# Hashed attention with two MLP layers: weight blocks converted and split in pairs of 1024 columns

## Chip, cores and metric

The kernel runs on one core of a Trainium2 chip. The metric is the device time of one launch in microseconds (us), the median of several runs. Engines are called TensorE (PE in the rows), VectorE (DVE), ScalarE (ACT), GpSimd (POOL) and SyncE (SP, whose queue issues all large DMAs here).

## What is computed

Attention in which a query sees only the keys of its hash bucket, then two MLP layers on the result. B, H, S, D are 2, 8, 768, 64; there are 6 hash bits, 1536 tokens, a model width of 512 and a hidden width of 2048.

```
q_bits = (q @ proj) > 0;  k_bits = (k @ proj) > 0
mask   = bucket(q_bits) == bucket(k_bits)
p      = softmax(where(mask, q @ k.T / sqrt(64), -1e9))
x      = heads_side_by_side(p @ v)                         # 1536 x 512
x      = relu(x @ w_in)**2 @ w_out                         # layer 0
h      = x @ w_in2
out    = (max(h, 0) + alpha * min(h, 0)) @ w_out2          # layer 1
```

The four weight matrices are float64 on the host and reach the kernel as their 64 bits.

## The kernel before

**Tiling.** Tokens are handled in NCH = 4 chunks of 384, and the hidden width in KFF = 16 steps of 128. A work item is a layer, a chunk and a step, 128 in all; `feed_forward` runs the 16 steps of a layer and chunk. A step needs two weight blocks of 128x512: block 0, from `w_in`, for the hidden product (`hidden`: 12 matmuls of 384 columns), and block 1, from `w_out`, for the projection (`project`: 9 matmuls of 512 columns). The projection of step f-1 is written behind the hidden product of step f. [...]

**The way of a weight block.** `load_bits` loads the raw 64-bit words as a tile `wbits` (two 32-bit words per value). `to_f32` makes float32 of it: ScalarE scales the high words into a tile `we` (L502), VectorE masks the sign into `wsg` (L504), adds bits of the low word (L505) and puts exponent and mantissa in place (L507). The result goes to a float32 tile `wf` (`fetch`, for layer 0 in its first chunk) or stays in `we` (`ahead`, for layer 1), and is stored to a scratch tensor in DRAM, from where later chunks load it again (L554). `split_w` then copies the high part on ScalarE (L528) and subtracts it on VectorE or GpSimd (L529). In layer 1 `keep` brings the blocks back into SBUF for good.

**Overlap.** Attention of the first chunk is computed first. Attention of chunk c+1 runs as background steps between the matmuls of layer 0 on chunk c, and the conversion of the layer 1 weights runs beside chunks 1 and 2 of layer 0. From about 480 us on there is no attention any more, only layer 0 on the last chunk and layer 1 (the late stage). In the attention each tile of scores is two pairs of matmuls into PSUM (L350, L351); VectorE takes its row maximum (L354), ScalarE the exponential (L357) that frees the PSUM tile. `recip` and `finish` scale the result by the row sums: `rrow` goes through DRAM and comes back as `rb`, and VectorE multiplies (`x`, L414), ScalarE makes `xh` (L415).

**What sets the order.** A list scheduler fixes, when the kernel is built, the order of instructions on each engine from the order of the code and its own estimates. At run time each engine and the SyncE queue work strictly in that order and wait on semaphores. A tile is taken from a pool with a fixed number of buffers; a new tile waits until the last reader of the buffer's earlier one is done. Pools that matter here: `whole` 4 (`wf`), `conv` 1 (`we` and `wsg`), `parts0` 2 and 3 in the late stage, `parts1` 2 (`wh`, `wl` of each block), `wide` 3 and 8 in the late stage (`wbits`, late `wf`).

**A step in the code.** `feed_forward` splits block 0 of the next item and block 1 of this one, computes the hidden product, fetches float32 weights two items ahead, loads raw bits three items ahead, and projects. GpSimd makes `wl` for each block 1 and, in the second chunk of layer 0, for block 0 too (`o or i // KFF == 1`); VectorE makes the rest.

Of the kernel before, what the change touches and what calls it, by code (L numbers as in the profile page):

```python
# [29 lines left out]
def kernel(  # L30
# [20 lines left out]
    nc = tc.nc  # L51
    B, H, D, S = qT.shape
    NB = N_BITS
    NT, DM = out.shape
    P = 128
    T = S // 2
# [20 lines left out]
    m2 = pool("m2", 2)  # L77
    state_whole = pool("whole", 4)
    weights = ctx.enter_context(ExitStack())
# [37 lines left out]
    def f32(ap):  # L117
        return ap.bitcast(F32)


    GR = 32
# [8 lines left out]
    def constants():  # L130
# [4 lines left out]
        with tc.tile_pool(name="once", bufs=1) as once:  # L135
            first = tc.keep_in_program_order
            cols = once.tile([P, D], i32, name="cols")
            row = once.tile([P, 1], i32, name="row")
            bit = once.tile([P, 1], i32, name="bit")
# [3 lines left out]
            sign = once.tile([P, D], F32, name="sign")  # L143
            nc.gpsimd.iota(row, [[0, 1]], base=0, channel_multiplier=1)
# [9 lines left out]
            first(nc.vector.tensor_tensor(of, of, above, ALU.mult))  # L154
            first(nc.vector.tensor_scalar(bit, row, GR // 2 - 1, None, ALU.bitwise_and))
            first(nc.vector.tensor_scalar(cols, cols, bit, 1, ALU.logical_shift_right, ALU.bitwise_and))
            first(nc.vector.tensor_scalar(sign, cols, 2.0, -1.0, ALU.mult, ALU.add))
# [6 lines left out]
            first(nc.vector.tensor_scalar(nb[:, 0, :], nb[:, 0, :], 1, None, ALU.bitwise_and))  # L164
            ones = once.tile([P, NB], F32, name="ones")
            first(nc.vector.tensor_copy(ones, nb[:, 0, :]))
# [38 lines left out]
    class Pair:  # L205
# [100 lines left out]
        def q_ids(self):  # L306
# [178 lines left out]
    w_d = {}  # L485
    kept = {}
    y_d = {}

    def load_bits(u):
        l, f, o = u  # L490
        t = state["wide"].tile([P, DM, 2], U32, tag="wide", name="wbits")
        nc.sync.dma_start(out=t.rearrange("p n b -> p (n b)"), in_=(WO if o else WI)[l][f].bitcast(U32))
        w_bits[u] = t

    def to_f32(u, w=None):


        if u not in w_bits:
            load_bits(u)
        t = w_bits.pop(u)  # L500
        e = state["conv"].tile([P, DM], F32, tag="we", name="we")
        nc.scalar.activation(e, t[:, :, 1].bitcast(F32), AF.Copy, scale=2.0 ** -112)  # L502
        s = state["conv"].tile([P, DM], U32, tag="wsg", name="wsg")
        nc.vector.tensor_scalar(s, t[:, :, 1], 0x80000000, None, ALU.bitwise_and)  # L504
        nc.vector.scalar_tensor_tensor(s, t[:, :, 0], 29, s, ALU.logical_shift_right, ALU.bitwise_or)  # L505
        w = e if w is None else w
        nc.vector.scalar_tensor_tensor(  # L507
            w.bitcast(U32), e.bitcast(U32), 3, s, ALU.logical_shift_left, ALU.bitwise_or
        )
        return w  # L510

    def ahead(u):

        w = to_f32(u)
        w_d[u] = dram.tile([P, DM], F32, tag="w%d_%d_%d" % u, name="w%d_%d_%d" % u)
        nc.sync.dma_start(out=w_d[u], in_=w)

    def keep(u):

        kept[u] = state["res"].tile([P, DM], F32, name="w%d_%d_%d" % u)  # L520
        nc.sync.dma_start(out=kept[u], in_=w_d[u])

    def split_w(u, engine):
        w = w_f.pop(u)
        o = u[2]
        hi = state["parts%d" % o].tile([P, DM], F32R, tag=f"wh{o}", name=f"wh{o}")
        lo = state["parts%d" % o].tile([P, DM], F32R, tag=f"wl{o}", name=f"wl{o}")
        nc.scalar.activation(hi, w, AF.Copy)  # L528
        engine.tensor_tensor(lo, w, f32(hi), ALU.subtract)  # L529
        w_split[u] = (hi, lo)  # L530
# [4 lines left out]
    def units(i):  # L535

        if i >= len(work):
            return []
        l, c, f = work[i]
        return [(l, f, o) for o in range(2)]  # L540

    def fetch(i):

        for u in units(i):
            if u in kept:
                w_f[u] = kept[u]
            elif u in w_d:
                if state["attention"]:
                    w = state["whole"].tile([P, DM], F32, tag="wf", name="wf")
                else:  # L550

                    w = state["wide"].tile([P, DM, 2], U32, tag="wide", name="wf")
                    w = w.rearrange("p n b -> p (n b)")[:, 0:DM].bitcast(F32)
                nc.sync.dma_start(out=w, in_=w_d[u])  # L554
                w_f[u] = w
            else:
                w_f[u] = state["whole"].tile([P, DM], F32, tag="wf", name="wf")
                to_f32(u, w_f[u])
                w_d[u] = dram.tile([P, DM], F32, tag="w%d_%d_%d" % u, name="w%d_%d_%d" % u)
                nc.sync.dma_start(out=w_d[u], in_=w_f[u])  # L560

    def split(i, o):
        for u in units(i)[o:o + 1]:
            split_w(u, nc.gpsimd if o or i // KFF == 1 else nc.vector)

# [58 lines left out]
    def feed_forward(l, c, background):  # L624
# [11 lines left out]
        for f in range(KFF):  # L636
            i = index[l, c, f]
            split(i + 1, 0)
            split(i, 1)
            g = hidden(l, c, f, x, step)  # L640
            fetch(i + 2)
            for u in units(i + 3):
                if u not in w_d and u[0] == 0:
                    load_bits(u)
# [60 lines left out]
    for f in range(KFF):  # L705
        for o in range(2):
            steps += [lambda u=(1, f, o): load_bits(u), lambda u=(1, f, o): ahead(u)]

# [97 lines left out]
```

## Time and profile before

| | us |
|---|---|
| median of 3 runs (lowest to highest) | 852.25 (851.3 to 853.84) |
| the profiled execution | 850.58 |
| its span in the trace | 848.8 |
| TensorE busy in the span | 798.8 (94%) |
| VectorE busy | 504.0 (59%) |
| ScalarE busy | 470.5 (55%) |
| GpSimd busy | 359.6 (42%) |

The profile is one execution, 1.67 us below the median of the runs; 1.8 us of it lie around the span. A row of the profile names a line of the kernel, the engine, the operation, the output and inputs with shapes, and a count. "Idle before" is the time for which the engine did nothing directly before an instruction, and the arrow names what ended it. The granted clock is the share of its full speed at which TensorE ran.

### The profile page before, as it was taken

The numbers are of one execution on the slowest core, as the hardware profiler recorded it, in microseconds if no ns is written. First come the engines' busy times: TensorE is split into PE (matmuls) and PEld (weight loads), VectorE is DVE, ScalarE is ACT, GpSimd is POOL, SyncE is SP. The second block draws the span as 40 slices with busy tenths as digits, with TensorE's granted clock in tenths as the row PEclk, the third lists the DMA queues.
The fourth block names the chain that finished last, engine by engine and source line by source line (L and its number), as shares of the span: only waits on it lengthen the run. The fifth ranks groups of instructions, "written<-read, shape, count | busy, mean of one in ns | idle before, by whom it ended". The sixth has DMA issues, their size and how long they took to land.

```text
span 848.8 us, 12785 instructions
## 1 busy us (share of the span) xinstructions
PE 798.8 (94%) x4384; PEld 648.0 (76%) x4384; DVE 504.0 (59%) x819; ACT 470.5 (55%) x919; POOL 359.6 (42%) x315
## 2 busy tenths in 40 slices
PE   3988799999999989999989999999999999999997
PEld 1656486767787666677677789989989998998996
DVE  6576789998567567788888431224435445444442
ACT  3566587777575655565565556654434443444332
POOL 1000232323555565533333355545555555555553
PEclk9999799999999999999999999999999999999999
DMA  7567767777867767778775489600101011000001
GB/s 206 153 174 214 226 229 249 239 252 249 228 215 215 236 192 240 234 245 257 241 219 170 120 310 314 233 29 10 38 1 37 1 38 38 1 1 37 1 1 38
DMA packets 62096, 130.09 MB, mean 153 GB/s; under 512 B 8816, under 2 KB 21072, under 8 KB 62032
## 3 DMA queue, kind: packets, MB, share of 16 engines
q1 hardware_dynamic: 62032, 129.28, 48.6%
q8 instruction: 35, 0.57, 0.3%
q14 instruction: 29, 0.24, 0.1%
HBM read 83.32 MB, written 23.12 MB: 125 GB/s over the span
## 4 chain that ended last, share of the span: by engine, by line
PE 48%; DVE 7%; DMA 3%; issue 2%; ACT 2%; POOL 1%; SPq 0%; POOLq 0%; DVEq 0%; ACTq 0%
PE acc L608 7%; PE acc L604 7%; PE acc L605 7%; PE m L578 4%; PE m L576 4%; PE m L577 4%; PE h L576 3%; PE h L577 3%; PE h L578 3%; PE m L387 3%; DMA w<-we 2%; DVE low L354 1%; DVE wsg L504 1%; DVE we L507 1%; DVE pt L377 1%
## 5 line engine op out<-in xcount | busy, mean ns | idle before, releaser
L594 POOL TENSOR_TENSOR gl<-g,gh 128x384 fp32r<-128x384 f32 x128 | 136.1, 1063 | 246.0 <-ACT gh L593 123.2
L604 PE MATMUL acc<-wh,gh 128*128 128x512 f32 x384 | 158.2, 412 | 0.0
L529 POOL TENSOR_TENSOR wl<-wf,wh 128x512 fp32r<-128x512 f32 x80 | 108.4, 1356 | 112.8 <-ACT wh L528 102.5
L605 PE MATMUL acc<-wl,gh 128*128 128x512 f32 x384 | 152.1, 396 | 0.0
L528 ACT ACTIVATE wh<-w 128x512 fp32r<-128x512 f32 x128 | 80.5, 629 | 80.8 <-PE m L577 45.6
L608 PE MATMUL acc<-wh,gl 128*128 128x512 f32 x384 | 115.8, 398 | 2.1 <-POOL gl L594 2.1
L528 ACT ACTIVATE wh<-wf 128x512 fp32r<-128x512 f32 x128 | 80.5, 630 | 64.8 <-PE h L577 24.2
L576 PE MATMUL h<-xh,wh 128*128 128x384 f32 x296 | 106.7, 360 | 4.6 <-ACT xh L415 3.2
L354 DVE TENSOR_REDUCE low<-s 128x1 f32<-128x768 f32 x84 | 80.1, 953 | 38.0 <-PE s L351 37.8
L577 PE MATMUL h<-xl,wh 128*128 128x384 f32 x296 | 101.6, 343 | 0.4 <-POOL xl L416 0.4
L578 PE MATMUL h<-xh,wl 128*128 128x384 f32 x296 | 101.5, 343 | 0.0
L357 ACT ACTIVATE sm<-s,low 128x768 f32<-128x768 f32 x84 | 75.6, 900 | 37.5 <-DVE low L354 37.1
L608 PEld LDWEIGHTS acc<-wh,gl 128*128 128x128 f32 x384 | 71.5, 188 | 21.3 <-POOL gl L594 5.0
L371 PE MATMUL m<-ident,sm 128*128 128x128 f32 x525 | 82.9, 276 | 4.0 <-ACT sm L357 1.8
L529 POOL TENSOR_TENSOR wl<-w,wh 128x512 fp32r<-128x512 f32 x64 | 82.7, 1291 | 6.0 <-ACT wh L528 6.0
L604 PEld LDWEIGHTS acc<-wh,gh 128*128 128x128 f32 x384 | 72.4, 189 | 15.9 <-issue 5.7
L605 PEld LDWEIGHTS acc<-wl,gh 128*128 128x128 f32 x384 | 72.5, 189 | 9.2 <-issue 0.6
L593 ACT ACTIVATE gh<-g 128x384 fp32r<-128x384 f32 x64 | 33.5, 524 | 81.7 <-DVE g L592 81.7
L591 DVE TENSOR_SCALAR r<-m,alpha_sb 128x384 f32<-128x384 f32 x43 | 26.6, 618 | 87.0 <-PE m L578 86.7
L371 PEld LDWEIGHTS m<-ident,sm 128*128 128x128 f32 x525 | 64.1, 141 | 18.5 <-ACT sm L357 3.0
L350 PE MATMUL s<-k,q 128*128 128x384 f32 x168 | 63.9, 380 | 12.6 <-ACT sm L357 10.6
L578 PE MATMUL m<-xh,wl 128*128 128x384 f32 x216 | 73.0, 338 | 0.5 <-DVE wl L529 0.5
(112 smaller groups left out, 1475.2 us busy)
## 6 DMA issues: line engine op xcount, KB each, us to landing
wf<-w SPq DMA_DIRECT2D x96, 256.0 KB
wbits<-in_w_in_dram SPq DMA_DIRECT2D x32, 512.0 KB
wbits<-in_w_out_dram SPq DMA_DIRECT2D x32, 512.0 KB
w<-wf SPq DMA_DIRECT2D x32, 256.0 KB
w<-we SPq DMA_DIRECT2D x32, 256.0 KB
w<-w SPq DMA_DIRECT2D x32, 256.0 KB
q<-qh SPq DMA_DIRECT2D x60, 96.0 KB
k<-kh SPq DMA_DIRECT2D x28, 192.0 KB
```

What stands on the lines that cost most here:

```text
L354: nc.vector.tensor_reduce(low, ps[:, 0:2, 0:HALF], AX.XY, ALU.max, negate=True)
L357: nc.scalar.activation(sm.rearrange("p (a n) -> p a n", a=2), ps[:, 0:2, 0:HALF], AF.Exp, bias=low, accum_out=self.sums[:, i:i + 1],)
L371: nc.tensor.transpose(ps[:, i * P:(i + 1) * P], pp[:, b * P:(b + 1) * P], ident)
L528: nc.scalar.activation(hi, w, AF.Copy)
L529: engine.tensor_tensor(lo, w, f32(hi), ALU.subtract)
L576: nc.tensor.matmul(hp, wih[:, ks], xh[:, kk, :], start=first, stop=False)
L577: nc.tensor.matmul(hp, wih[:, ks], xl[:, kk, :], start=False, stop=False)
L578: nc.tensor.matmul(hp, wil[:, ks], xh[:, kk, :], start=False, stop=last)
L594: nc.gpsimd.tensor_tensor(gl, g, f32(gh), ALU.subtract)
L604: nc.tensor.matmul(acc[:, t, :], gh[:, blocks[t]], woh, start=first, stop=False)
L605: nc.tensor.matmul(acc[:, t, :], gh[:, blocks[t]], wol, start=False, stop=False)
L608: nc.tensor.matmul(acc[:, t, :], gl[:, blocks[t]], woh, start=False, stop=last)
```

## The change

Block 1 of item i and block 0 of item i+1 become one pair, held in one tile of 128x2x512.

- `to_f32` and `wh` work on 1024 columns in one operation: 31 conversions of pairs and two of single blocks, 126 `wh` copies of pairs and four of single blocks. The subtractions for `wl` stay 512 columns wide, the second half of the tile (block 0 of i+1) first.
- There is no tile `we`. ScalarE scales the high words in place in `wbits`, and VectorE's first operation reads them after that. A result of `ahead` stays in `wsg` and is stored from there.
- Fetching is one item ahead and not two, raw bits two and not three. Loads and stores are as many and as large as before.
- Pools hold pairs: `whole` 2, `parts` 2 (early and late), `wide` 2 and 8 late, `conv` one `wsg`.
- `ql` is written over `qn`, and three tiles of `constants` over others.

Lines of the changed kernel: L505 scaling, L507, L508 and L510 the three VectorE operations, L578 `wh`, L585 `wl`, L352 the row maximum, L412 `x`, L401 `rrow`, L615 `gh`.

```diff
-    state_whole = pool("whole", 4)
+    state_whole = pool("whole", 2)
...
-        state["parts0"] = pool(f"parts0{late}", 2 + late, stack)
-        state["parts1"] = pool(f"parts1{late}", 2, stack)
-        state["wide"] = pool(f"wide{late}", 8 if late else 3, stack)
+        state["parts"] = pool(f"parts{late}", 2, stack)
+        state["wide"] = pool(f"wide{late}", 8 if late else 2, stack)
...
-            ql = p1.tile([P, T], F32R, tag="ql", name="ql")
+            ql = self.qn.bitcast(F32R)
...
+    def load_bits(us):
+        t = state["wide"].tile([P, 2, DM, 2], U32, tag="wide", name="wbits")
+        for k, (l, f, o) in enumerate(us):
+            nc.sync.dma_start(
+                out=t[:, k].rearrange("p n b -> p (n b)"), in_=(WO if o else WI)[l][f].bitcast(U32)
+            )
+        w_bits[us] = t
+
+    def to_f32(us, w=None):
...
+        e = t[:, 0:n, :, 1]
+        nc.scalar.activation(e.bitcast(F32), e.bitcast(F32), AF.Copy, scale=2.0 ** -112)
+        s = state["conv"].tile([P, 2, DM], U32, tag="wsg", name="wsg")[:, 0:n]
+        nc.vector.tensor_scalar(s, e, 0x80000000, None, ALU.bitwise_and)
+        nc.vector.scalar_tensor_tensor(s, t[:, 0:n, :, 0], 29, s, ALU.logical_shift_right, ALU.bitwise_or)
+        w = s if w is None else w.bitcast(U32)
+        nc.vector.scalar_tensor_tensor(w, e, 3, s, ALU.logical_shift_left, ALU.bitwise_or)
+        return w.bitcast(F32)
+
+    def store(us, w):
+        for k, u in enumerate(us):
+            w_d[u] = dram.tile([P, DM], F32, tag="w%d_%d_%d" % u, name="w%d_%d_%d" % u)
+            nc.sync.dma_start(out=w_d[u], in_=w[:, k])
+
+    def ahead(us):
+        store(us, to_f32(us))
...
+    def fetch(i):
+        us = blocks_of(i)
...
+        ring = "whole" if state["attention"] else "wide"
+        w = state[ring].tile([P, 2, DM], F32, tag=ring, name="wf")
+        new = bits_of(i)
+        if len(new) == 2:
+            to_f32(us, w)
+            store(us, w)
...
+    def split(i):
+        us = blocks_of(i)
+        w, parts = w_f.pop(i)
+        hi = state["parts"].tile([P, 2, DM], F32R, tag="wh", name="wh")
+        lo = state["parts"].tile([P, 2, DM], F32R, tag="wl", name="wl")
+        if parts is None:
+            nc.scalar.activation(hi, w, AF.Copy)
...
+        for k, u in reversed(list(enumerate(us))):
+            engine = nc.gpsimd if u[2] or i // KFF == 1 else nc.vector
+            engine.tensor_tensor(lo[:, k], parts[k], f32(hi[:, k]), ALU.subtract)
...
-            split(i + 1, 0)
-            split(i, 1)
+            split(i)
             g = hidden(l, c, f, x, step)
-            fetch(i + 2)
-            for u in units(i + 3):
-                if u not in w_d and u[0] == 0:
-                    load_bits(u)
+            if i + 1 < len(work):
+                fetch(i + 1)
+            if i + 2 < len(work) and bits_of(i + 2) and state["attention"]:
+                load_bits(bits_of(i + 2))
...
+    fetch(-1)
     fetch(0)
-    fetch(1)
-    split(0, 0)
+    split(-1)
```

The change moves instructions in three places. First, VectorE ahead of the first `x` of the MLP (behind the last `rrow` of the first chunk); before:

```order
L529 TENSOR_TENSOR wl_1028<-wf,wh_1027 128x512
L504 TENSOR_SCALAR wsg<-wbits 128x512
L505 SCALAR_TENSOR_TENSOR wsg<-wbits,wsg 128x512
L507 SCALAR_TENSOR_TENSOR wf<-we,wsg 128x512
L504 TENSOR_SCALAR wsg<-wbits 128x512
L235 TENSOR_SCALAR bits<-m 128x96
L505 SCALAR_TENSOR_TENSOR wsg<-wbits,wsg 128x512
L235 TENSOR_SCALAR bits<-m 128x96
L507 SCALAR_TENSOR_TENSOR wf<-we,wsg 128x512
L504 TENSOR_SCALAR wsg<-wbits 128x512
L505 SCALAR_TENSOR_TENSOR wsg<-wbits,wsg 128x512
L414 TENSOR_TENSOR x<-u,rb 128x384
```

After, from that `rrow` on:

```order
L401 COPY rrow<-m 6x128
L585 TENSOR_TENSOR wl<-wf,wh 128x512 x2
L507 TENSOR_SCALAR wsg<-wbits 128x1024
L508 SCALAR_TENSOR_TENSOR wsg<-wbits,wsg 128x1024
L233 TENSOR_SCALAR bits<-m 128x96
L510 SCALAR_TENSOR_TENSOR wf<-wbits,wsg 128x1024
L316 SCALAR_TENSOR_TENSOR qn<-qn,qh 128x384
L233 TENSOR_SCALAR bits<-m 128x96
L412 TENSOR_TENSOR x<-u,rb 128x384
```

Eleven operations of 512 columns and less ahead of `x` have become eight, three of them of 1024 columns, with the write of `ql` (here named `qn`) moved behind `rrow`.

Second, VectorE in a background conversion of layer 1 weights during the second chunk, with what each operation waits for; before:

```order
L403 COPY rrow<-m 6x128 [waits PE_49]
L504 TENSOR_SCALAR wsg<-wbits 128x512 [waits DMAHW5_49]
L505 SCALAR_TENSOR_TENSOR wsg<-wbits,wsg 128x512 [waits DVE_49]
L507 SCALAR_TENSOR_TENSOR we<-we,wsg 128x512 [waits DMAHW2_49,DVE_49,Activation_49]
L354 TENSOR_REDUCE low<-s 128x1 [waits PE_49]
L235 TENSOR_SCALAR bits<-m 128x192 [waits PE_49]
```

After:

```order
L352 TENSOR_REDUCE low<-s 128x1 [waits PE_49]
L412 TENSOR_TENSOR x<-u,rb 128x384 [waits DMAHW5_49,DMAHW6_49,Activation_49,Pool_49]
L507 TENSOR_SCALAR wsg<-wbits 128x1024 [waits DMAHW1_49,DMAHW3_49,DMAHW0_49,Activation_49]
L508 SCALAR_TENSOR_TENSOR wsg<-wbits,wsg 128x1024 [waits DVE_49]
L510 SCALAR_TENSOR_TENSOR wsg<-wbits,wsg 128x1024 [waits DVE_49]
L375 COPY pt<-m 128x384 [waits PE_49]
```

The whole set of three, on a pair, still stands in one piece; the result is left in `wsg` and not in `we`, and the first operation now waits for ScalarE's scaling as well as for DMAs.

Third, ScalarE in the late stage, one step being two or three rows; before:

```order
L528 ACTIVATE wh_8406<-w_11_1_6682 128x512
L528 ACTIVATE wh_8478<-w_14_0_6812 128x512
L593 ACTIVATE gh<-g 128x384
L528 ACTIVATE wh_8444<-w_12_1_6734 128x512
L528 ACTIVATE wh_8516<-w_15_0_6854 128x512
L593 ACTIVATE gh<-g 128x384
L528 ACTIVATE wh_8482<-w_13_1_6776 128x512
L528 ACTIVATE wh_8554<-w_0_0_6122 128x512
```

After:

```order
L578 ACTIVATE wh<-w_6268 128x1024
L615 ACTIVATE gh<-g 128x384
L578 ACTIVATE wh<-w_5632 128x1024
L615 ACTIVATE gh<-g 128x384
L578 ACTIVATE wh<-w_5651 128x1024
```

Two copies of 512 columns and `gh` per step have become one copy of 1024 and `gh`.

## Rows read from the trace of the kernel before

**Rows 1.** Stretches: length, busy per engine (instructions), granted clock, DMA share, GB/s.

```profile
96.20:106.40 10.20, 6.95 (x19) 5.86 (x20) 5.62 (x9) 4.58 (x9) 2.01 (x2) 0.50 0.75 208
106.40:215.00 108.60, 104.68 (x608) 80.00 (x608) 97.77 (x157) 82.06 (x169) 32.96 (x27) 1.00 0.75 241
215.00:480.00 265.00, 253.49 (x1482) 194.08 (x1478) 192.63 (x296) 161.38 (x324) 125.07 (x103) 1.00 0.71 219
480.00:843.00 363.00, 360.40 (x1816) 321.09 (x1816) 140.78 (x235) 165.46 (x301) 189.88 (x167) 1.00 0.20 67
```

**Rows 2.** TensorE's waits, 104 to 480 us: total us, times, longest (first and last).

```profile
PE s L350 <- ACT sm L357: 9.3, 13, 1.4
...
PE m L371 <- ACT u L393: 0.2, 1, 0.2
```

**Rows 3.** Timeline around 330 us: start, duration, engine, line, operation, idle before.

```profile
329.83 3.15 POOL L529 TENSOR_TENSOR wl<-wf,wh 128x512 fp32r<-128x512 f32 x2
...
330.19 1.66 DVE L505 SCALAR_TENSOR_TENSOR wsg<-wbits,wsg 128x512 uint32<-128x512 uint32 x1
...
331.77 0.94 DVE L354 TENSOR_REDUCE low<-s 128x1 f32<-128x768 f32 x1
...
333.80 0.44 PE L350 MATMUL s<-k,q 128*128 128x384 f32 x1 [1.43 <-ACT sm L357]
```

**Rows 4.** Operations on the tile of raw bits: count, ns minimum/median/maximum.

```profile
L504 DVE TENSOR_SCALAR wsg<-wbits x64: 383/427/1510, 56.9 to 465.4; 128x512 uint32<-128x512 uint32 x64
L505 DVE SCALAR_TENSOR_TENSOR wsg<-wbits,wsg x64: 649/693/1667, 57.3 to 465.8; 128x512 uint32<-128x512 uint32 x64
```

**Rows 5.** Groups by form: busy us, mean ns | idle before, its releasers.

```profile
L528 ACT ACTIVATE wh<-wf 128x512 fp32r<-128x512 f32 x128 | 80.5, 630 | 64.8 <-PE h L577 24.2 <-PE acc L608 21.4 <-PE m L577 9.1
...
L505 DVE SCALAR_TENSOR_TENSOR wsg<-wbits,wsg 128x512 uint32<-128x512 uint32 x64 | 49.7, 777 | 1.5
...
L502 ACT ACTIVATE we<-wbits 128x512 f32<-128x512 f32 x64 | 43.2, 676 | 36.0 <-DMA w<-we 16.6 <-DVE wf L507 14.5 <-DMA wbits<-in_w_in_dram 2.5
L504 DVE TENSOR_SCALAR wsg<-wbits 128x512 uint32<-128x512 uint32 x64 | 41.1, 642 | 15.7 <-DMA wbits<-in_w_out_dram 9.2 <-DMA wbits<-in_w_in_dram 5.9
...
L585 ACT ACTIVATE gh<-r 128x384 fp32r<-128x384 f32 x64 | 33.5, 523 | 1.7
...
L507 DVE SCALAR_TENSOR_TENSOR wf<-we,wsg 128x512 uint32<-128x512 uint32 x32 | 27.9, 873 | 2.7 <-POOL wl L529 0.6 <-DVE wsg L505 0.6 <-ACT wh L528 0.4
...
L507 DVE SCALAR_TENSOR_TENSOR we<-we,wsg 128x512 uint32<-128x512 uint32 x32 | 26.0, 813 | 12.7 <-ACT we L502 12.2
...
L152 DVE TENSOR_SCALAR above<-of 128x8 f32<-128x8 f32 x1 | 0.2, 156 | 0.0
```

**Rows 6.** Waits of SyncE's DMA queue over the span.

```profile
SPq L554 <- POOL wl L529: 50.0, 33, 3.5
```

**Rows 7.** Groups of instructions from 104 to 480 us: the exponential.

```profile
L357 ACT ACTIVATE sm<-s,low 128x768 f32<-128x768 f32 x72 | 64.8, 900 | 26.9 <-DVE low L354 26.5
```

**Rows 8.** Timeline of one late step, from 650 us.

```profile
650.24 0.62 DVE L591 TENSOR_SCALAR r<-h,alpha_sb 128x384 f32<-128x384 f32 x1 [1.88 <-PE h L578]
...
650.78 1.05 DVE L529 TENSOR_TENSOR wl<-w,wh 128x512 fp32r<-128x512 f32 x1
...
652.12 0.33 PE L576 MATMUL m<-xh,wh 128*128 128x384 f32 x1
...
652.33 0.53 ACT L593 ACTIVATE gh<-g 128x384 fp32r<-128x384 f32 x1 [1.63 <-DVE g L592]
...
654.23 0.39 PE L604 MATMUL acc<-wh,gh 128*128 128x512 f32 x1
```

**Rows 9.** TensorE's waits, 480 to 849 us (first of three).

```profile
PE acc L608 <- POOL gl L594: 1.8, 5, 0.4
```

**Rows 10.** Timeline ahead of the first hidden product.

```profile
97.13 0.55 DVE L414 TENSOR_TENSOR x<-u,rb 128x384 f32<-128x384 f32 x1
...
98.29 0.69 PE L576 MATMUL h<-xh,wh 128*128 128x384 f32 x1 [3.20 <-ACT xh L415]
```

More of the change, by code (lines that the diff above doesn't have):

```diff
@@ L138, in constants @@
             row = once.tile([P, 1], i32, name="row")
-            bit = once.tile([P, 1], i32, name="bit")
             nb = once.tile([P, 2, NB], i32, name="nb")
@@ L142, in constants @@
             of = once.tile([P, 2 * NG], F32, name="of")
-            sign = once.tile([P, D], F32, name="sign")
+            sign = cols.bitcast(F32)
             nc.gpsimd.iota(row, [[0, 1]], base=0, channel_multiplier=1)
@@ L164, in constants @@
             first(nc.vector.tensor_scalar(nb[:, 0, :], nb[:, 0, :], 1, None, ALU.bitwise_and))
-            ones = once.tile([P, NB], F32, name="ones")
+            ones = nb[:, 1, :].bitcast(F32)
             first(nc.vector.tensor_copy(ones, nb[:, 0, :]))
@@ L486 @@
     kept = {}
+    here = {}
     y_d = {}
-    def load_bits(u):
-        l, f, o = u
[L491 to L498, printed above, removed]
-            load_bits(u)
[L500 to L530, printed above, removed]
+    def load_bits(us):
[5 more added lines that the diff above has]
+        w_bits[us] = t
@@ new lines, in to_f32 @@
+    def to_f32(us, w=None):
+        if us not in w_bits:
+            load_bits(us)
+        n = len(us)
+        t = w_bits.pop(us)
+        e = t[:, 0:n, :, 1]
[6 more added lines that the diff above has]
+        return w.bitcast(F32)
@@ new lines, in store, with keep @@
+    def store(us, w):
[4 more added lines that the diff above has]
+        store(us, to_f32(us))
+    def keep(u):
+        l, f, o = u
+        g = f if o else (f - 1) % KFF
+        if g not in kept:
+            kept[g] = state["res"].tile([P, 2, DM], F32, name=f"w{g}")
+        nc.sync.dma_start(out=kept[g][:, 1 - o], in_=w_d[u])
+        here[u] = kept[g][:, 1 - o]
@@ L532 @@
     work = [(l, c, f) for l in range(2) for c in range(NCH) for f in range(KFF)]
     index = {w: i for i, w in enumerate(work)}
[L535 to L540, printed above, removed]
-    def fetch(i):
[L544 to L555, printed above, removed]
-            else:
[L557 to L560, printed above, removed]
@@ L562, in split, with blocks_of, bits_of @@
-    def split(i, o):
-        for u in units(i)[o:o + 1]:
-            split_w(u, nc.gpsimd if o or i // KFF == 1 else nc.vector)
+    def blocks_of(i):
+        u = []
+        if 0 <= i:
+            u.append((work[i][0], work[i][2], 1))
+        if i + 1 < len(work):
+            u.append((work[i + 1][0], work[i + 1][2], 0))
+        return tuple(u)
+    def bits_of(i):
+        return tuple(u for u in blocks_of(i) if u not in w_d and u not in here)
+    def fetch(i):
+        us = blocks_of(i)
+        if all(u in here for u in us):
+            if len(us) == 2:
+                w_f[i] = (kept[us[0][1]], None)
+            else:
+                w_f[i] = (None, [here[us[0]]])
+            return
+        ring = "whole" if state["attention"] else "wide"
[4 more added lines that the diff above has]
+            store(us, w)
+        else:
+            for k, u in enumerate(us):
+                if u in new:
+                    to_f32((u,), w[:, k:k + 1])
+                    store((u,), w[:, k:k + 1])
+                elif u in w_d and u not in here:
+                    nc.sync.dma_start(out=w[:, k], in_=w_d[u])
+        w_f[i] = (w, None) if len(us) == 2 and not any(u in here for u in us) else (
+            None, [here[u] if u in here else w[:, k] for k, u in enumerate(us)]
+        )
@@ L705 @@
     for f in range(KFF):
-        for o in range(2):
-            steps += [lambda u=(1, f, o): load_bits(u), lambda u=(1, f, o): ahead(u)]
+        us = ((1, f, 0), (1, f, 1))
+        steps += [lambda us=us: load_bits(us), lambda us=us: ahead(us)]
     conversion = Background(steps, [(1.0, 0), (NCH - 1.1, len(steps))])
```

11 lines of the change are left out of this document (8 added, 3 removed).

## Prediction

> **What bounds the kernel now.** I first read the table by stretch, which gives TensorE's busy time, its granted clock and the other engines' load. Four stretches matter. From 480 us on only matrix work is left: 360.4 us of 363 are busy, so 2.6 us can be won there. From 215 to 480 us 11.5 us of 265 are idle, and from 106.4 to 215 us 3.9 us of 108.6; there VectorE is busy 97.8 us of the 108.6. [...] All other time is matrix work that the change leaves alone. So it can give back at most 11.5 + 3.9 + 2.6 + (3.25 idle and some 3.5 of half-clock work) = 25 us of 850.58, the profiled run, of which the trace spans 848.8.
>
> Then I read who ends these idle times. Between 104 and 480 us nine groups of TensorE waits sum to 14.8 us; the first and largest, 13 waits and 9.3 us, is a score matmul (L350) that waits for the exponential (L357) of an earlier block to free its PSUM tile [rows 2]. The exponential waits for a row reduction (L354) on VectorE. The timeline at 330 us shows why that one is late: a conversion operation (L505) of 1.66 us stands directly ahead of the reduction, beside a GpSimd subtraction; the reduction starts at 331.77 and the scores at 333.80 after 1.43 us of waiting [rows 3]. The same operation takes 693 ns in the median and 1667 at the most, L504 427 and 1510 [rows 4]: the excess, about 1 us, goes with GpSimd's work. Nine such stalls that I followed one by one (from 178 to 437 us) have the same shape: a conversion operation of 1.0 to 1.7 us ahead of the reduction, or ScalarE held in L502. L502 itself waits 36.0 us, 16.6 for the store that still reads `we` and 14.5 for the VectorE operation that does [rows 5].
>
> **The change part by part.** *Conversion on VectorE.* Before, 64 sets of three operations: 41.1 + 49.7 + 27.9 + 26.0 = 144.7 us [rows 5]. After, 31 sets of 1024 columns and two of 512. An operation of 8 columns takes 0.156 us [rows 5], taken as the part that does not grow, so a 1024-column scalar-tensor-tensor costs 2 x 0.693 - 0.156 = 1.23 us. For the first operation I take 0.70 (2 x 0.427 - 0.156), and as stretching by GpSimd 0.45 a set: before it was 2.26 (144.7 / 64) less the medians 0.427 + 0.693 and once more 0.693 [rows 4], also 0.45, but for twice as many sets. A set is 0.70 + 1.23 + 1.23 + 0.45 = 3.6 us and the sum 31 x 3.6 + 2 x 2.26 = 116 us: 28 us less on VectorE. VectorE is not the bound on average, so none of this counts by itself; it counts where an operation stands ahead of a reduction, an `x` or an `r`. The subtractions stay 512 columns wide and as many.
>
> [...]
>
> *ScalarE.* The 256 `wh` copies of 512 columns become 126 of 1024 and four of 512, the 64 scalings 31 and two. 384 columns take 523 ns and 512 take 630 [rows 5], so 0.83 ns a column and 1.06 us for 1024. Each merged pair saves 0.2 us, (126 + 31) x 0.2 = 31 us of ScalarE busy time, nearly all of it beside TensorE's work. The scaling is now strided and in place on `wbits`, which no row of before shows. The bounds are 1.06 (the slope) and 1.35 us (two of L502's 676 ns [rows 5]); I take 1.2. It goes ahead of the first VectorE operation, which so far ran beside it: that wait is hidden when the scheduler has other VectorE work, and costs up to 1.2 us on VectorE when it stands ahead of a reduction.
>
> *One buffer less.* There is no `we` tile any more; L502's 31.1 us of waits for it have no cause left. In exchange, an ahead-of-time result stays in `wsg`, and the next set's first VectorE operation waits for its store. What is then queued behind on VectorE is a reduction, and behind that an exponential and scores. Bound: nothing, as there are 16 such steps instead of 32, twice as far apart, up to the 16.6 us that ScalarE waited for the store before [rows 5]. Of the 26.5 us that exponentials waited for reductions [rows 7] 9.3 reached TensorE [rows 2], a third. So the bound on the path is 0 to 5 us; I take 1, near the low end, since the steps are twice as far apart.
>
> *Fetch one step ahead, two pair buffers.* The queue on SyncE waited 50.0 us for GpSimd's subtraction before it could load into a buffer, and TensorE had no wait for such a load [rows 2, 6]. A pair is free when both its subtractions are done, and a step in the attention stage takes some 8 us ((480 - 98) / 48). I take nothing; the cover is that step's length, and if it goes, each step pays the load in full.
>
> *Late stage (from 480 us).* The copies of step i+1 now wait for the projection that last reads the pair. In the step at 650 us `r` starts at 650.24, `gh` is written at 652.33 to 652.86 and first read at 654.23, with 1.4 us to spare; the subtraction at 650.78 takes 1.05 us and stands ahead of `g` [rows 8]. After the change `r` and `g` follow each other, so `gh` is done near 652.0, then comes one copy from 652.1 (the projection is over, the next hidden product begins) to 653.2 or 653.5, then the subtractions to 654.1 or 654.8. The next hidden product but one reads them at 654.23 + 2.1 = 656.3: some 1.5 us to spare. So no new stall, and `gl`, which caused 1.8 of the 2.6 us of waits (three groups) [rows 9], comes earlier: -1.
>
> *First MLP step.* TensorE waits 3.2 us for `xh` at 98.29, since `x` runs only at 97.13 [rows 10], with eleven VectorE operations of conversion, splitting and hashing directly ahead of it. In the changed order eight stand there: two of 512 columns (1.4), a set of 1024 (0.70 + 1.23 + 1.23) and `ql` and two `bits`, which at 0.156 to 0.55 each, the ends being the 8-column operation and `x` itself, I take at 1.0: 5.6 us against eleven for some 6.5 to 8 before. The wait for the pair's bits can take all of that back. I put `x` 0 to 2 us earlier: -1.
>
> *Sum.* The loop's 14.8 us of waits [rows 2]: the causes are either stretched conversion operations, now half as many, or the `we` buffer. Counted over VectorE's whole order, a conversion operation stands directly ahead of 39 of the 96 reductions before and of 27 after, 76 operations (some 46 us at the medians) against 45 (some 47 us): fewer places by a third, the same work in them, half the stretching. I take a third off, -5, between none and all. Against it, what stands ahead of a reduction is 1.23 instead of 0.69 us: for some four of 72 score tiles at 0.5 us each one pays 2, with the store's 1 it is +3; in a third of these places a stall that I leave standing covers it, so +2. Together -5 - 1 - 1 + 2 = -5, or 845.6 for a run like the profiled one. That run lay 1.67 us below the median of the runs, 852.25, so the forecast is **847.5**.
>
> **The rivals.** *Slower: long operations that cannot be broken off.* Place: the reduction of the 72 score tiles of chunks 1 to 3. Each L505 or L507 ahead of one is 0.54 us longer, and the scaling's wait can come on top; a set back to back is 3.2 us instead of 1.8. Nine tiles at 0.54 cancel the 5 us, 14 more at 0.4 make it slower by 0.3%; with 25 to 36 of the 72 tiles hit, the time is 855 to 860. For it: VectorE is 90% busy from 106 to 215 us [rows 1]; 13 stalls have this shape already [rows 2]. Against it: total VectorE work falls, and the places fall from 39 to 27. [...] Chance 0.15. *A starved late stage:* if the copy or the subtraction in the late steps takes over 1.5 us more than I put, every one of some 80 steps pays the rest; 0.1 us each is +8, 856. Chance 0.05, since [rows 8] leave 1.5 us.
>
> *No change:* the 14.8 us trade places, since a stall that is taken away lets TensorE run on to the next late reduction; or the operations never were the cause and the exponentials set the pace (0.90 us on ScalarE for each [rows 7]). 851 to 853. The same follows if the change does not do what it says, the subtractions staying 512 wide and being what stretches. Chance 0.25.
>
> *A larger gain:* all loop waits and the half-clock stretch go: 14.8 + 3.5, or 834 to 838. It needs every reduction to be on time, which 27 places don't give. Chance 0.07.
>
> **How the numbers follow.** About 0.3% (2.5 us) is what a measurement of this kernel can tell from no change, so "same" is 849.7 to 854.8. Forecast, 840 to 849.7: 0.48. With the larger gain, faster has 0.55, same 0.25, slower 0.15 + 0.05 = 0.20. The range leaves out the larger gain and the upper part of the slower cases: 839 to 857. Both signs hold chances, but faster has most; its own range is 840 to 849.7.
>
> **What would show it.** Right, if VectorE's conversion falls from 144.7 to about 116 us, the group of scores waiting for the exponential to some 6 us with fewer than 13 waits, the late stretch keeps at least 360 us busy in 363, and `x` stands before 97. Wrong: the group grows past 12 us with an L508 or L510 of over 1.2 us ahead of the reduction (the slower rival); a first conversion operation that waits for the store of `wsg`; a late `hidden` matmul that waits for `wh` or `wl` step after step; or unchanged waits under new names (no change).

## The result and the profile after

The changed kernel takes 860.06 us in the median of 8 runs (856.52 to 863.44), the kernel before 852.52 beside it: a ratio of 1.0099 with a 95% interval of 1.0077 to 1.0121. It is slower by 1%, where 847.5 us had been forecast, and outside the range. The profiled execution took 856.52 us, 3.5 us below its median, so the trace shows a little less of the loss than the runs do. Single executions of one kernel lie up to 9 us apart here; below, the runs decide and a trace only shows how.

VectorE's conversion fell as forecast. By form, in the profile after (busy us, mean ns, then idle time before them and what ended it):

```profile
L508 DVE SCALAR_TENSOR_TENSOR wsg<-wbits,wsg 128x1024 uint32<-128x1024 uint32 x31 | 42.7, 1377 | 0.6
...
L507 DVE TENSOR_SCALAR wsg<-wbits 128x1024 uint32<-128x1024 uint32 x31 | 25.8, 832 | 18.3 <-ACT wbits L505 15.1 <-DMA w<-wsg 3.2
L510 DVE SCALAR_TENSOR_TENSOR wsg<-wbits,wsg 128x1024 uint32<-128x1024 uint32 x16 | 21.0, 1315 | 0.2
L510 DVE SCALAR_TENSOR_TENSOR wf<-wbits,wsg 128x1024 uint32<-128x1024 uint32 x15 | 19.8, 1321 | 0.1
```

With the two single blocks (3.6 us) that is 112.9 us after 144.7 [rows 5]. New are 15.1 us in which VectorE waits for ScalarE's scaling. The subtractions, which make `wl` of a weight block and `wh`, its copied high part, grew, although their shape is the same; the tile `wl` (count, ns minimum/median/maximum) between 104 and 482 us, after, and behind it GpSimd's part of it from 482 us on:

```profile
L585 POOL TENSOR_TENSOR wl<-wf,wh x59: 1263/1293/3019, 105.5 to 475.7; 128x512 fp32r<-128x512 f32 x59
L585 DVE TENSOR_TENSOR wl<-wf,wh x27: 649/796/1784, 106.8 to 476.1; 128x512 fp32r<-128x512 f32 x27
```

```profile
L585 POOL TENSOR_TENSOR wl<-w,wh x64: 1289/1802/1816, 571.4 to 843.6; 128x512 fp32r<-128x512 f32 x64
```

Before, the median of VectorE's was 684 ns in the attention stage, and that of GpSimd's late ones 1291. The stretches that answer to [rows 1], after (the same times, so not quite the same work):

```profile
96.20:106.40 10.20, 9.67 (x43) 8.80 (x43) 6.22 (x7) 6.29 (x12) 5.69 (x4) 0.76 0.73 223
106.40:215.00 108.60, 103.02 (x622) 80.28 (x620) 88.78 (x119) 79.34 (x144) 36.81 (x27) 1.00 0.75 238
215.00:480.00 265.00, 246.41 (x1433) 190.55 (x1431) 185.12 (x250) 153.98 (x273) 128.46 (x102) 1.00 0.70 217
480.00:843.00 363.00, 358.61 (x1801) 316.91 (x1800) 153.29 (x234) 156.15 (x220) 230.34 (x166) 1.00 0.20 68
```

The first MLP step came out better than forecast, with a granted clock of 0.76 instead of 0.50. From 215 to 480 us TensorE is busy 7.1 us less, and GpSimd is busy 40 us more in the late stage. TensorE's waits of 104 to 482 us (total, times, longest), the first four:

```profile
PE s L348 <- ACT sm L355: 9.8, 13, 1.6
PE h L600 <- POOL wl L585: 3.9, 4, 2.9
PE m L369 <- DVE pt L375: 3.2, 4, 1.5
PE m L399 <- DVE rin L397: 2.3, 3, 1.2
```

The group of [rows 2] did not shrink (13 times, 9.3 us before, 9.8 now), three groups came up beside it, and all groups together went from 14.8 to 24.0 us. One of the places, ScalarE around 260 us (start, duration, operation, idle time before and its releaser):

```profile
260.67 1.15 ACT L505 ACTIVATE wbits<-wbits 128x1024 f32<-128x1024 f32 x1 [2.99 <-DMA wbits<-in_w_out_dram]
261.72 1.05 ACT L578 ACTIVATE wh<-wf 128x1024 fp32r<-128x1024 f32 x1
262.67 0.88 ACT L355 ACTIVATE sm<-s,low 128x768 f32<-128x768 f32 x1
```

ScalarE waits 2.99 us for the second block's raw bits, and a copy and an exponential are queued behind; the reduction had ended at 259.9, and a score matmul waits 1.20 us for the exponential.

The late stage is best read by two matmuls, the first hidden product of layer 0's last chunk and that of the last step of all; first before, then after:

```profile
498.14 0.33 PE L576 MATMUL m<-xh,wh 128*128 128x384 f32 x1
...
836.31 0.33 PE L576 MATMUL m<-xh,wh 128*128 128x384 f32 x1
```

```profile
500.53 0.33 PE L598 MATMUL m<-xh,wh 128*128 128x384 f32 x1
...
842.55 0.33 PE L598 MATMUL m<-xh,wh 128*128 128x384 f32 x1
```

338.2 us became 342.0: a loss of 3.8 us in a stage for which a gain of 1 had been forecast. The loop ahead of it, from the hidden product that waits for the last `xh` of the first MLP step (98.29 us before [rows 10], 94.05 after, shown below) to these first products, took 399.9 us before and 406.5 after: 6.6 us lost, where a gain of 3 had been forecast. The first MLP step itself came 4.2 us earlier.

### The profile page after: what moved, and what is told of

Its sections match the earlier page's. It is cut to its first block, busy times and chain, and to the rows that moved or that the text cites. A ratio compares the mean times of both kernels' runs of the same rounds, so it can differ in the third digit from the quotient of the medians.

```text
span 854.7 us, 12384 instructions
## 1 busy us (share of the span) xinstructions
PE 797.3 (93%) x4384; PEld 649.9 (76%) x4384; DVE 498.7 (58%) x726; ACT 453.9 (53%) x762; POOL 413.7 (48%) x315
## 5 line engine op out<-in xcount | busy, mean ns | idle before, releaser
L616 POOL TENSOR_TENSOR gl<-g,gh 128x384 fp32r<-128x384 f32 x128 | 139.5, 1090 | 151.3 <-ACT gh L615 64.7
L585 POOL TENSOR_TENSOR wl<-wf,wh 128x512 fp32r<-128x512 f32 x80 | 126.2, 1588 | 143.3 <-ACT wh L578 125.1
L585 POOL TENSOR_TENSOR wl<-w,wh 128x512 fp32r<-128x512 f32 x64 | 112.7, 1761 | 33.2 <-ACT wh L578 32.5
L585 DVE TENSOR_TENSOR wl<-w,wh 128x512 fp32r<-128x512 f32 x64 | 48.9, 764 | 116.3 <-ACT wh L578 112.7
L352 DVE TENSOR_REDUCE low<-s 128x1 f32<-128x768 f32 x84 | 80.1, 954 | 60.8 <-PE s L349 60.3
L615 ACT ACTIVATE gh<-g 128x384 fp32r<-128x384 f32 x64 | 33.7, 527 | 127.5 <-DVE g L614 127.5
L578 ACT ACTIVATE wh<-wf 128x1024 fp32r<-128x1024 f32 x63 | 66.6, 1058 | 24.0 <-PE acc L630 14.3
L578 ACT ACTIVATE wh<-w 128x1024 fp32r<-128x1024 f32 x63 | 66.9, 1063 | 21.7 <-PE acc L630 18.4
L585 DVE TENSOR_TENSOR wl<-wf,wh 128x512 fp32r<-128x512 f32 x48 | 43.4, 903 | 54.1 <-ACT wh L578 41.8
```

The source lines that it names most:

```text
L352: nc.vector.tensor_reduce(low, ps[:, 0:2, 0:HALF], AX.XY, ALU.max, negate=True)
L585: engine.tensor_tensor(lo[:, k], parts[k], f32(hi[:, k]), ALU.subtract)
L616: nc.gpsimd.tensor_tensor(gl, g, f32(gh), ALU.subtract)
```

## Experiments

All ratios are to the kernel before, run beside, with their 95% interval. Each kernel has one trace. In the attention stage traces differ by some us (the changed kernel and `e_late_sep`, alike up to there, reach the last chunk at 500.5 and 505.6 us), so totals are taken from the runs. The late stage repeats: between the two matmuls above it takes 342.0 to 342.4 us in all seven traces with the merged copy there, and 337.7 to 338.2 in all eleven with separate tiles and copies of 512 columns, so it is taken from the traces.

**Which part: length of operations, or coupled blocks?** Three theories stood at the start: the 1024-column operations are too long ("length", the slower rival of the prediction), the two blocks of a pair hold each other up ("coupling"), or GpSimd's double work in the second chunk. Everything on 512 columns, pair tiles kept (`e_all512`):

```diff
-        nc.scalar.activation(e.bitcast(F32), e.bitcast(F32), AF.Copy, scale=2.0 ** -112)
+        for k in range(n):
+            nc.scalar.activation(e[:, k].bitcast(F32), e[:, k].bitcast(F32), AF.Copy, scale=2.0 ** -112)
...
-            nc.scalar.activation(hi, w, AF.Copy)
...
         for k, u in reversed(list(enumerate(us))):
+            nc.scalar.activation(hi[:, k], parts[k], AF.Copy)
```

> The changed kernel with its pair tiles, pools and fetching as they are, but every operation on a pair cut in two of 512 columns (scaling, the three VectorE operations, the copy to wh). Theory 'length' (1024-column operations that stand ahead of reductions and of the copies cost the time): about the kernel before, 852 to 855 us. Theory 'coupling' (a pair's buffer is held for two blocks, so copies, subtractions and loads come just in time): stays at 858 to 861. Theory 'GpSimd' (in the second chunk both subtractions of a pair go to GpSimd one behind the other): stays at 858 to 861.

Measured 861.29 us, 1.0122 (1.0092 to 1.0152). The loss stays without any long operation, so "length" alone does not carry it, as far as one order of the work can say (an edit can make the scheduler order the whole work anew, and further down a new order alone moves 0.8%).

Separate tiles for `wh` and `wl` (`e_sep`), and the same with conversion on 512 columns (`e_sep512`):

```diff
-        hi = state["parts"].tile([P, 2, DM], F32R, tag="wh", name="wh")
...
-            nc.scalar.activation(hi, w, AF.Copy)
...
+            hi = state["parts%d" % o].tile([P, DM], F32R, tag=f"wh{o}", name=f"wh{o}")
...
+            nc.scalar.activation(hi, parts[k], AF.Copy)
```

> The changed kernel with wh and wl of each block in their own tiles again (pools of 2 and 2, late 3 and 2) and copies of 512 columns; conversion stays on pairs with 1024 columns. 'Coupling': 852 us or below, as the saved VectorE time then shows. 'Length' of the conversion: 857 to 860; if the length of the copy is what counts, 852 to 854. 'GpSimd': about 858.

> As e_sep, and the conversion too by operations of 512 columns, so that of the change only the pair tiles for raw bits and float32 weights, the fetch order, the in-place scaling and the in-place ql are left. 'Coupling' and 'length' both: 851 to 854. If it is still 857 or more, neither the operations nor the wh/wl tiles are the cause, but the fetch order, the in-place scaling or ql.

Measured 860.0 us, 1.0110 (1.0078 to 1.0143), and 854.91 us, 1.0041 (1.0019 to 1.0063). Short operations alone (`e_all512`) gain nothing, separate tiles and copies alone (`e_sep`) gain nothing, both together gain 5 us: none of the three theories says that.

Block 0's subtraction in the second chunk on VectorE (`e_dve`):

```diff
-            engine = nc.gpsimd if u[2] or i // KFF == 1 else nc.vector
+            engine = nc.gpsimd if u[2] else nc.vector
```

> The changed kernel, in the second chunk of layer 0 with block 0's subtraction on VectorE and not on GpSimd. 'GpSimd': the loss of 4.2 us in that chunk goes, 854 to 856. 'Coupling' and 'length': 858 to 862, as VectorE gets 16 operations of 0.7 us more.

Measured 856.91 us, 1.0067 (1.0043 to 1.0090): some 2.7 us less than the change (0.0032 x 852), near the 3.9 us of TensorE's waits for `wl`, though the two intervals overlap. In the traces the second chunk's 16 steps (from the first hidden product of the one chunk to that of the next) take 145.3 us in the changed kernel and 144.8 here, against 141.2 before, so the loss there did not go.

**Late bits, and each merge alone.** In `e_early` the next pair's raw bits are loaded ahead of this pair's conversion:

```diff
+    steps = [steps[0]] + [s for f in range(KFF) for s in (steps[2 * f + 2:2 * f + 3] + steps[2 * f + 1:2 * f + 2])]
```

> The changed kernel with one edit: in the background conversion of the layer 1 weights the raw bits of the next pair are loaded ahead of the conversion of this one (the order of two background steps swapped). Theory 'late bits' (ScalarE's scaling waits for a whole pair's loads, 17 us in all between 104 and 482 us, with an exponential queued behind it): these waits fall below 6 us, and the time to 854 to 857 us. Theories 'coupling' and 'length': 858 to 861, as TensorE's waits have other causes.

Measured 858.7 us, 1.0101 (1.0067 to 1.0135). ScalarE's waits from 104 to 482 us for raw bits fell from 17.0 us to 7.8 (under 6 had been expected), and the time did not follow:

```profile
ACT wbits L505 <- DMA wbits<-in_w_in_dram: 4.8, 5, 1.6
...
ACT wbits L505 <- DMA wbits<-in_w_out_dram: 3.0, 4, 1.9
```

So the stall at 260 us is a true one, but not what the 1% hangs on. `e_we` undoes the conversion and the split, `e_pair_we` the conversion alone, `e_wh512` the merged copy alone:

```diff
+            e = state["conv"].tile([P, DM], F32, tag="we", name="we")
+            nc.scalar.activation(e, t[:, k, :, 1].bitcast(F32), AF.Copy, scale=2.0 ** -112)
+            s = state["conv"].tile([P, DM], U32, tag="wsg", name="wsg")
...
```

> As e_sep512, with the conversion as before the change in all points: tiles we and wsg of 512 columns, results ahead of time left in we. What is left of the change is pair tiles for raw bits and float32 weights, the fetch order and the in-place ql. If the in-place scaling and the store from wsg cost the remaining 4 us of e_sep512: 850 to 852. If the tiles and the fetch order do: 854 to 856.

> The changed kernel with wh and wl pairs and merged copies, but the conversion as before the change (512 columns, tiles we and wsg). 'Coupling': 857 to 861, as in the changed kernel. 'Length' of the conversion's operations or 'late bits': 851 to 854, but for the some 3 us that the late stage loses with merged copies: 854 to 856.

> The changed kernel with only the wh copy cut in two of 512 columns, block 0 first, in the same pair tile; conversion on 1024 columns. If the merged copy releases both subtractions at once, so that GpSimd and VectorE stretch each other, the layer 1 stage gives back its 2 us: 857 to 858 if nothing else changes. 'Coupling': 859 to 862.

Measured 852.38 us, 1.0019 (1.0005 to 1.0033); 861.44 us, 1.0120 (1.0077 to 1.0163); 862.59 us, 1.0138 (1.0116 to 1.0160). What is left in `e_we` (fetch order, pair tiles for loads, `ql` in place) costs next to nothing in the total. Either merge alone (the copies in `e_pair_we`, the conversion in `e_wh512` and `e_sep`) costs 1% or more, both together cost no more than one, and with the pair tiles left and neither merge (`e_all512`) it is 1.2% too.

`e_wh512` misses its number but settles the late stage: from the first hidden product at 509.97 us to that of the last step at 848.82 its trace has 338.9 us, the same as `e_all512` (510.54 to 849.41), against 342.0 with the merged copy and 338.2 before. So of 3.8 us the merged copy costs 3.1, and holding both blocks in one buffer 0.7.

**The late stage undone, and a control of the order.** `e_late_sep` goes back to separate tiles and 512-column copies when the attention has ended. The two controls of the kernel before and the one of the change shift only when the background conversion runs:

```diff
+        if not state["attention"]:
...
+            for k, u in reversed(list(enumerate(us))):
...
+                hi = state["parts%d" % o].tile([P, DM], F32R, tag=f"wh{o}", name=f"wh{o}")
...
+                nc.scalar.activation(hi, parts[k], AF.Copy)
...
-    conversion = Background(steps, [(1.0, 0), (NCH - 1.1, len(steps))])
+    conversion = Background(steps, [(1.1, 0), (NCH - 1.1, len(steps))])
```

> The changed kernel, from the last chunk of layer 0 on with wh and wl in a tile for each block again (pools 3 and 2) and copies of 512 columns; until then the change as it is. Theory 'late pairs' (merged copies cost 3.3 us from 480 us on): TensorE's waits there become those of the kernel before, and the time 855 to 857 us against 851 of before. If the late stage only moves its waits: 858 to 861.

> The kernel before, with the background conversion of the layer 1 weights starting at 1.1 chunks and not at 1.0 (same end, same operations). Control for theory 'order' (any new order of the same work is some us worse or better, and the change mostly draws another order in the attention stage): 848 to 860, off by more than 2.5 us. Theory 'operations' (the changed operations themselves cost the time): 850 to 853.

> The kernel before, with the background conversion ending at 2.8 chunks and not at 2.9 (same start, same operations). 'Order': 848 to 860, and not the same as with the later start. 'Operations': 850 to 853.

> The changed kernel, with the background conversion starting at 1.1 chunks. 'Order': differs from the changed kernel by more than 2.5 us, either way. 'Operations': 858 to 861.

Measured: `e_late_sep` 853.82 us, 1.0047 (1.0024 to 1.0071), 0.5% below the change; its late stage takes 337.7 us (505.6 to 843.3). `p_before_a` 852.62 us, 1.0020 (0.9998 to 1.0043); `p_before_b` 854.39 us, 1.0037 (1.0015 to 1.0058). `p_after_a` 852.68 us, 1.0017 (0.9998 to 1.0036): a start one tenth of a chunk later, with the same operations, takes 0.8% off the changed kernel, where in the kernel before it gives nothing. "Order" is right for the change. For the kernel before, the later start (0.2%, an interval that takes in none) stays below the 2.5 us that it expected, and the earlier end, at 0.37% or 3.1 us, lies just above.

**Is it the start?** `p_after_b` keeps the start at 1.0 and ends at 2.8, `p_after_c` starts at 1.2 (same line as above). `late_sep_a` joins the start at 1.1 with the late stage of `e_late_sep`, and `late_sep_dve_a` adds the edit of `e_dve`.

> The changed kernel with the background conversion from 1.0 to 2.8 chunks and not to 2.9. 'Bad start' (pairs that begin at 1.0 collide with the end of layer 0's own conversion): 857 to 861 us, as in the changed kernel. 'Order' (any new order lands elsewhere): off the changed kernel by over 2.5 us.

> The changed kernel with the background conversion from 1.2 to 2.9 chunks. 'Bad start': 851 to 854 us, as with 1.1. 'Order': anywhere from 848 to 862, by no rule of the start.

> Two edits of the changed kernel together: separate tiles and 512-column copies in the late stage, and the start at 1.1. If the late loss (3.9 us by the profiles) and the loss in the attention stage add: 847 to 850, below both kernels. If they overlap: 851 to 853.

> As late_sep_a, and in the second chunk block 0's subtraction on VectorE. 'GpSimd' (its double share there costs 3 us in any order): 1 to 3 us below late_sep_a. 'Order': above or below it.

Measured: 862.37 us, 1.0141 (1.0106 to 1.0176); 854.17 us, 1.0036 (1.0015 to 1.0058); 847.81 us, 0.9941 (0.9913 to 0.9968); 846.25 us, 0.9938 (0.9917 to 0.9958). Two starts at 1.0 are slow and two later ones are not, as "bad start" says. The traces show where: the second chunk's 16 steps take 139.5 to 141.2 us in all six traces of the change and its variants with a later start, and 142.7 to 154.8 in all eleven with the start at 1.0. The kernel before does not follow this: 141.2, and 144.7 with the later start (`p_before_a`). The two losses add up (1.0099 less 0.0052 and 0.0082 is 0.9965), and without them the pairs beat the kernel before by 0.6% and the changed one by 1.6%. By the trace of `late_sep_a` that gain is the first MLP step's and not the loop's: the hidden product that waits for `xh` runs at 94.71 us (before: 98.29), and from there to the last chunk it takes 401.1 us, against 399.9 before and 401.9 and 399.0 in `p_before_a` and `p_before_b`. The scores wait for the exponential 13 times there too:

```profile
PE s L352 <- ACT sm L359: 9.0, 13, 1.5
```

The third edit adds nothing that can be told from `late_sep_a`. TensorE's waits from 482 us on, of `late_sep_dve_a`, are again nearly those of the kernel before [rows 9]:

```profile
PE acc L645 <- POOL gl L631: 1.8, 5, 0.4
PE m L613 <- ACT wh L585: 0.3, 1, 0.3
```

**What the merges are worth there.** `best_conv512` cuts the conversion of `late_sep_dve_a` into 512 columns, `best_sep` gives `wh` and `wl` separate tiles and copies in the attention stage too (edits as in `e_all512` and `e_sep`).

> late_sep_dve_a with the conversion cut into operations of 512 columns (scaling and the three VectorE operations), all else alike. If fewer, longer operations save what stands ahead of reductions and x: 849 to 853 us against 846. If VectorE's saved time is off the path: 845 to 848.

> late_sep_dve_a with wh and wl in a tile for each block and copies of 512 columns in the attention stage too; conversion on 1024 columns. If the merged copy stretches subtractions there and costs time: 842 to 845. If ScalarE's saved time is worth more: 849 or above. If neither: 845 to 848.

Measured 852.8 us, 1.0028 (1.0010 to 1.0047), and 850.87 us, 1.0002 (0.9984 to 1.0020). Taken away from the good version, each merge costs: the conversion 0.9% (some 7.7 us), the copies, together with the pair tiles for `wh` and `wl`, 0.6% (some 5.5 us). Both edits also order the work anew, and each was tried in one order only; in the traces `best_sep` even gains 2.8 us up to the second chunk's first hidden product and loses 5.4 in the third chunk. How much of the two numbers is the merge and how much the order is not shown.

## Why the prediction was wrong

**What bounds the kernel, and the saving on VectorE:** in the bound of 25 us, the 3.25 idle and some 3.5 of half-clock work are the first stretch of [rows 1]. Right as far as busy time goes: conversion went to 112.9 us (116 forecast). That this saving buys time where conversion stands ahead of a reduction did not show, as the sum over the loop below tells. `best_conv512` lost 7.7 us by short operations, in one order, and its trace puts 1.7 us of that on the first MLP step.

**The first MLP step:** right in kind, undersized. `x` ran at 92.89 us (95 to 97 forecast), and the hidden product waited 1.96 us instead of 3.20 [rows 10], 4.2 us earlier than before:

```profile
92.89 0.55 DVE L412 TENSOR_TENSOR x<-u,rb 128x384 f32<-128x384 f32 x1
...
94.05 0.59 PE L598 MATMUL h<-xh,wh 128*128 128x384 f32 x1 [1.96 <-ACT xh L413]
```

The eight operations took 5.6 us, as forecast, with 1.5 us of idle time. What was mis-sized is the other side: the eight are counted from the last `rrow`, the eleven of before from a subtraction further on. From `rrow` at 87.08 us on, fifteen operations of 10.0 us stood ahead of `x`. Nor does the gain need the merges: in `e_we`, which undoes them, twelve stand there, and the hidden product runs at 94.45 us.

**Late stage:** this step failed. It priced the merged copy by its duration, 1.06 us, which is what it takes (1063 ns in the mean), and found 1.5 us to spare in a step at 650 us, a regular one. It did not ask what the copy waits for and what it releases, nor look at the other steps. It waits for both blocks of a pair, so at the entry to the stage, where loads arrive just in time, it comes late; and it releases both subtractions in one moment, on VectorE and GpSimd, of which one then takes longer. The entry in the profile after, by engine:

```profile
502.88 1.06 ACT L578 ACTIVATE wh<-wf 128x1024 fp32r<-128x1024 f32 x1 [0.83 <-DMA w<-w]
...
504.02 1.80 POOL L585 TENSOR_TENSOR wl<-wf,wh 128x512 fp32r<-128x512 f32 x1 [5.27 <-ACT wh L578]
...
503.97 0.69 DVE L585 TENSOR_TENSOR wl<-wf,wh 128x512 fp32r<-128x512 f32 x1 [1.20 <-ACT wh L578]
...
503.99 0.45 PE L598 MATMUL m<-xh,wh 128*128 128x384 f32 x1 [0.76 <-ACT wh L578]
...
511.47 0.50 PE L627 MATMUL acc<-wl,gh 128*128 128x512 f32 x1 [1.01 <-POOL wl L585]
```

The reader sees the copy wait for a load, both subtractions start within 0.1 us of its end, GpSimd's take 1.80 instead of 1.29 us, and TensorE wait for the copy and, at 511.47, for a subtraction. In the regular steps the 1.5 us did suffice: most take 4.19 us before and after. The 16 steps of layer 0's last chunk lose 1.7 us, of which `e_wh512` gives back 0.9, and the steps behind them 2.15, of which it gives back all. Nearly all of the 2.15 lies at the four joints, where one chunk ends and the next begins: there the copy waits for a hidden product that still reads, both subtractions come late, and `gl` stands behind GpSimd's. The joint at 645 us:

```profile
644.31 1.06 ACT L578 ACTIVATE wh<-w 128x1024 fp32r<-128x1024 f32 x1 [0.67 <-PE h L599]
...
645.45 1.29 POOL L585 TENSOR_TENSOR wl<-w,wh 128x512 fp32r<-128x512 f32 x1 [2.93 <-ACT wh L578]
645.62 1.67 DVE L585 TENSOR_TENSOR wl<-w,wh 128x512 fp32r<-128x512 f32 x1
...
646.69 1.47 POOL L616 TENSOR_TENSOR gl<-g,gh 128x384 fp32r<-128x384 f32 x1
...
648.22 0.96 PE L630 MATMUL acc<-wh,gl 128*128 128x512 f32 x3 [0.23 <-POOL gl L616]
```

All waits of TensorE from 482 us on, after:

```profile
PE acc L630 <- POOL gl L616: 2.5, 9, 0.3
PE acc L627 <- POOL wl L585: 1.0, 1, 1.0
PE m L598 <- ACT wh L578: 0.8, 1, 0.8
PE h L598 <- ACT wh L578: 0.3, 1, 0.3
```

The term was -1 and measured +3.8 in the trace; undoing it gave 0.5% in the runs.

**The sum over the loop:** the term -5 + 2 failed as a whole: the trace lost 6.6 us there. The prediction counted conversion operations ahead of reductions and took the waits to fall with them; the count fell from 39 to 27 and the waits of scores stayed at 13. It also took the order of before as given: with the background conversion starting at 1.0 the changed order lost some 7 us (1.0099 against 1.0017 with the start at 1.1), and the count does not show such a difference. But the 5 us did not come with the better start either: in `late_sep_a` the scores still wait 13 times and 9.0 us and the loop is no shorter than before. In no variant did this group fall to the forecast 6 us; 7.6 (`e_pair_we`) is the least.

What goes wrong at the start of 1.0 stays open. Late raw bits alone do not carry it (`e_early`), nor long operations alone (`e_all512`), nor a single one of the merges (`e_pair_we` and `e_sep`, each slow with one of them), as far as one order each can say. One difference is seen: in the changed kernel the queue issues the two loads of the second background pair at 247.89 and 255.22 us, in `p_after_a` directly behind each other:

```profile
262.17 0.46 SPq L492 DMA_DIRECT2D wbits<-in_w_in_dram  x1
262.67 0.43 SPq L492 DMA_DIRECT2D wbits<-in_w_out_dram  x1
```

By itself it does not carry the loss either: `e_early`, which starts at 1.0 and is as slow as the change, issues the two nearly as close together:

```profile
248.29 0.43 SPq L492 DMA_DIRECT2D wbits<-in_w_in_dram  x1
249.07 0.33 SPq L492 DMA_DIRECT2D wbits<-in_w_out_dram  x1
```

**The rivals.** The slower side came true, not by long operations ahead of reductions (0.15), but by a late stage held up by copy and subtraction, near the rival that had 0.05, and by the order in the attention stage, which no rival named. The sum of the first rival is off: 14 tiles at 0.4 us are 5.6 us or 0.7%, not 0.3%. That a subtraction takes longer beside one on the other engine did show, in the rows above: at the entry VectorE's starts first and takes 0.69 us, and GpSimd's takes 1.80; at the joint GpSimd's starts first and takes 1.29 us, and VectorE's takes 1.67. The later one ends 1.16 and 0.55 us after the first, a little less than the medians of late subtractions, 1.29 us on GpSimd before and 0.69 on VectorE after. But in the late stage it is the pair of subtractions of unchanged length that meet, not longer conversions. The rival "no change" was right that the score waits would stay; the waits of all groups did not trade places, they grew.

**Buffers and fetching:** taken at nothing. `e_we`, which keeps them and undoes both merges, bears that out in the total (0.2%), but in its trace the total is made of two parts: the first MLP step comes 3.8 us earlier and the loop takes 406.2 us, 6.4 longer. So what is left there moves time in both places, as far as one trace can say.

## What to carry to other kernels

The merged copy waited for the last of its inputs (0.83 us for a load at the entry) and released its readers at once (two subtractions 0.05 us apart, one of 1.80 us instead of 1.29): price what a merged operation waits for and what then runs side by side, not only what it saves by itself (here 1.06 us against two of 0.63). Where a scheduler places background work, shift its start by a tenth before judging a change; here that was worth nearly as much as the change, and it is also the size of what a single edit can seem to gain or lose. And judge a merge stage by stage, at the entry and the joints too: merged copies cost 3.1 us behind the attention, where regular steps hid them, and what they gain beside it was not told apart from the order.

## What was not expected of the hardware

The same subtraction of 128x512 took 684 to 693 ns on VectorE in the median, from 104 to 482 us, in six kernels in which each block has a copy of its own, and 796 to 1166 ns in four in which one copy releases both (the changed kernel the least, `e_dve` the most). In the late stage it was GpSimd's that grew, from 1291 to 1802 ns in the median, and VectorE's only from 681 to 693; at the four joints after, where GpSimd's starts first, it is the other way round: 1.29 us on GpSimd and 1.67 on VectorE.

Around stalls of nearly 3 us the granted clock fell in one kernel and not in another: in `e_sep`, with TensorE waits of 2.70 us up to 220.14 and of 2.60 us up to 348.56, it was 0.91 in the mean of both of these stretches of 40 us, and in the changed kernel, with 2.94 us of waiting up to 341.77, 1.00. What decides between the two no run here shows; first `e_sep`, then the changed kernel:

```profile
200.00:240.00 40.00, 36.67 (x199) 27.48 (x198) 25.34 (x36) 20.07 (x40) 11.87 (x8) 0.91 0.58 162
320.00:360.00 40.00, 35.34 (x177) 27.51 (x175) 23.88 (x27) 21.99 (x42) 23.79 (x19) 0.91 0.66 216
```

```profile
320.00:360.00 40.00, 35.45 (x202) 26.15 (x201) 20.64 (x29) 20.95 (x37) 25.23 (x20) 1.00 0.64 207
```
